# Band matrices summed into the weights' layout, and three batches convolved and transposed by halves, in a convolution and soft-mixture kernel

## The chip, the cores and the metric

One Trainium2 chip, one of its cores. The metric is the device time of one execution in microseconds (us); less is better. The kernel before was timed three times.

## The reference, cut to what matters

```python
# x [8, 3584, 192], weight [8 heads, 7], phi [192, 32], w1 [8, 192, 1024], w2 [8, 1024, 192], all float32
w = softmax(weight, axis=-1)
out = np.einsum('hk,bskhg->bshg', w, x_unf)     # causal convolution of 7 rows, one filter for each 24 channels
x = out.reshape(28672, 192)
logits = x @ phi
d = softmax(logits, axis=0)                     # over all 28672 rows
slot_input = (d.T @ x).reshape(8, 4, 192)
slot_out[e] = np.maximum(slot_input[e] @ w1[e], 0.0) @ w2[e]
c = softmax(logits, axis=1)
return c @ slot_out.reshape(32, 192)
```

## The kernel before

**The stages.** The eight batches of x (2.75 MB each) are loaded one after the other into five buffers, xs0 to xs4, each as 128 partitions x 32 windows x 192 channels; batches 5 to 7 take the buffers of batches 0 to 2. TensorE convolves a batch in place: a window of 128 rows gives 2 x 56 outputs, by a matmul with a band matrix `toep` (partitions x heads x 64) into PSUM, and ScalarE (ACT) or VectorE (DVE) copies the result back over x ("evacuation", L181 or L185). DVE transposes the convolved batch in six blocks of 32 channels into `xt` (L457, L504), TensorE multiplies the blocks by phi into the logits (L526, accumulated over the six blocks in `lg0` and `lg1`), DVE copies the logits out and takes their maximum (L541 to L556), ACT makes the exponentials (L567), TensorE turns them (L598) and multiplies them with the batch (L620, "dispatch"). The batches go through this in the groups [0], [1, 2], [3, 4], [5, 6], [7]. Beside it w1 and w2 are loaded into buffers that have come free, and the row softmax (L651 to L679) runs in gaps on POOL (GpSimd), DVE and ACT. After the last group comes the small two-layer network (L782 to L883), then the output: matmuls (L912), evacuation, and 22 MB of stores.

**The band matrix (L319 to L389).** The softmax of the weights is taken on DVE (L335 to L341). `shf` holds ones shifted along 32 columns. For each half of the heads a product of 128 x 1064 is taken (L363, one half on DVE, the other on POOL), summed over the 7 taps by DVE into a band of 4 heads x 38 columns (L366), and eight small copies by ACT, DVE or POOL put pieces of the band into `toep` (L382).

**The halo copies (L304 to L309).** Eight partitions of every quarter of a batch are copied from partitions 64 to 71 by POOL or ACT (L181, L183), in two pieces for batches 0 and 1 and in one piece for the others.

**The convolution.** `conv` (L425) takes one head at a time over the whole batch, with the two PSUM pairs cv0 and cv1 in turn. `conv_halves` (L461) is used for batch 0 alone: half of the batch (quarters 0 and 1, then 2 and 3) and two heads at a time, with four PSUM pairs; behind each half come two transposes of three blocks each (L504). `xt` has six blocks for the first batch of a group and three for the second, whose blocks 3 to 5 are written over its blocks 0 to 2 after their logits.

**The order of the work.** Every step is given to a planner (`Plan`) with a cost, what it reads and writes, and a priority; it walks through the steps by these costs, chooses an engine where several are allowed, and puts out the instructions of each engine in that order. On the chip every engine then runs its own list in order. Loads are issued by SP in order; `load` lets each wait for an earlier one, so that at most `most` bytes are under way:

```python
most = 1900000 if b < 2 else 1600000
```

Four dummy matmuls (L400) keep TensorE busy before the first convolution.

## Time and profile before

| what | value |
|---|---|
| time, median of 3 runs | 209.65 us (208.44 to 210.06) |
| the profiled execution: its own time | 209.57 us |
| its span, first to last instruction | 207.7 us |
| busy: PE, DVE, ACT, POOL | 168.5, 153.4, 96.5, 101.9 us |
| DMA | 60.16 MB, mean 290 GB/s |
| mean granted clock of TensorE | 0.929 |

The span lies inside the profiled execution's own time; what is around it is 1.87 us. In the trace every float32 matmul stands as two records, so an "x32" of matmuls is 16 matmuls.

### The profile page before, as it was taken

What the parts mean: (1) busy time and instruction counts of PE and PEld (TensorE: products, weight loads), DVE (VectorE), ACT (ScalarE), POOL (GpSimd) and SP (SyncE); (2) the same over time, 40 slices, a digit from 0 to 9 for tenths busy, and PEclk for the clock granted to TensorE, in tenths of its full rate; (3) what the DMA queues carried; (4) which work ended last, traced back from release to release, by engine and by line L of the source; (5) the groups of instructions that cost most, each with busy time, mean ns of one, the idle gap of its engine ahead of it and who ended that gap; (6) DMA issues with size and microseconds to landing.
All of it is one profiled execution on the core that took longest, in us unless ns stands there. A gap on an engine that the chain in (4) does not pass through costs nothing.

```text
span 207.7 us, 6742 instructions
## 1 busy us (share of the span) xinstructions
PE 168.5 (81%) x2816; PEld 102.0 (49%) x2816; DVE 153.4 (74%) x236; ACT 96.5 (46%) x163; POOL 101.9 (49%) x115
## 2 busy tenths in 40 slices
PE   4776699999899998999998989899899996729000
PEld 2255545323254362443643557657698896618000
DVE  6999648888799887998689995975587797555100
ACT  3557237453665506848038423140497876424000
POOL 8854336566464654560800035776668668740000
PEclk9999579999999999999999999999999999685855
DMA  4999999999999989758786887880199999999994
GB/s 118 333 319 318 284 299 275 322 299 327 295 312 303 303 254 304 212 174 278 245 252 218 246 266 246 260 264 3 42 328 391 411 412 407 407 413 411 413 417 203
DMA packets 47806, 60.16 MB, mean 290 GB/s; under 512 B 2848, under 2 KB 41632, under 8 KB 47776
## 3 DMA queue, kind: packets, MB, share of 16 engines
q1 hardware_dynamic: 47776, 59.73, 86.9%
q8 instruction: 22, 0.36, 0.7%
q14 instruction: 8, 0.07, 0.1%
HBM read 37.70 MB, written 22.02 MB: 288 GB/s over the span
## 4 chain that ended last, share of the span: by engine, by line
PE 41%; DMA 30%; DVE 8%; POOL 4%; ACT 4%; issue 3%; SPq 1%; POOLq 1%; DVEq 0%; ACTq 0%
DMA xs<-in_x_dram 25%; PE cv L436 10%; PE lg L526 7%; PE cv L620 5%; PE cv L912 4%; PE lg L598 4%; DMA out_dram<-xs 3%; PE lg L620 3%; PE lg L866 3%; ACT xs L181 3%; PE lg L912 2%; DMA xs<-in_moe_w_dram 2%; DVE xs L185 2%; PE cv L826 2%; POOL eall L663 2%
## 5 line engine op out<-in xcount | busy, mean ns | idle before, releaser
L181 ACT COPY xs<-cv 128x768 f32<-128x768 f32 (+1 forms) x60 | 46.2, 796 | 57.1 <-PE cv L436 29.3
L183 POOL COPY xs<-xs 8x1536 f32<-8x1536 f32 (+1 forms) x32 | 41.4, 1297 | 34.3 <-DMA xs<-in_x_dram 32.7
L457 DVE STREAM_TRANSPOSE xt<-xs 128x1024 f32<-128x1024 f32 x42 | 49.0, 1214 | 1.6 <-issue 0.8
L436 PE MATMUL cv<-xs,toep 64*64 64x384 f32 x448 | 44.4, 500 | 3.8 <-ACT xs L181 2.1
L185 DVE COPY xs<-cv 128x768 f32<-128x768 f32 (+1 forms) x32 | 29.8, 939 | 13.1 <-PE cv L912 6.6
L663 POOL TENSOR_TENSOR eall<-eall,rms 128x896 f32<-128x896 f32 x16 | 26.9, 1698 | 24.1 <-DVE rms L651 17.1
L526 PE MATMUL lg<-xt,phi 32*32 32x448 f32 (+1 forms) x960 | 30.0, 512 | 3.2 <-DVE xt L504 2.5
L912 PE MATMUL cv<-so,eall 32*128 32x192 f32 x248 | 25.2, 460 | 8.0 <-DVE eall L671 7.2
L436 PEld LDWEIGHTS cv<-xs,toep 64*64 64x64 f32 x448 | 13.2, 131 | 28.5 <-ACT xs L181 11.1
L912 PEld LDWEIGHTS cv<-so,eall 32*128 32x128 f32 x248 | 20.5, 317 | 10.5 <-issue 7.8
L526 PEld LDWEIGHTS lg<-xt,phi 32*32 32x32 f32 x960 | 15.1, 109 | 15.1 <-issue 4.8
L912 PE MATMUL lg<-so,eall 32*128 32x192 f32 x200 | 20.6, 433 | 0.0
L671 DVE STREAM_TRANSPOSE eall<-eall 128x896 f32<-128x896 f32 x16 | 17.4, 1096 | 2.1 <-POOL eall L663 1.9
L912 PEld LDWEIGHTS lg<-so,eall 32*128 32x128 f32 x200 | 18.1, 319 | 0.5 <-ACT xs L181 0.3
L654 POOL TENSOR_TENSOR tree<-eall 128x448 f32<-128x448 f32 x8 | 9.2, 1149 | 13.6 <-ACT eall L675 13.6
L185 DVE COPY xs<-lg 128x768 f32<-128x768 f32 (+2 forms) x24 | 12.8, 558 | 3.1 <-PE lg L846 2.0
L541 DVE TENSOR_SCALAR_CACHE_REDUCE eall<-lg 128x448 f32<-128x448 f32 x16 | 9.1, 621 | 7.6 <-PE lg L526 7.6
L181 ACT COPY xs<-lg 128x768 f32<-128x768 f32 (+1 forms) x20 | 13.6, 707 | 1.9 <-PE lg L912 1.6
L675 ACT ACTIVATE eall<-eall 128x896 f32<-128x896 f32 x8 | 7.6, 955 | 10.8 <-POOL eall L663 10.6
L620 PE MATMUL cv<-xs,dn 128*32 128x192 f32 x256 | 11.5, 328 | 1.1 <-issue 0.7
L620 PE MATMUL lg<-xs,dn 128*32 128x192 f32 x256 | 11.6, 328 | 0.3 <-ACT dn L181 0.3
L658 POOL TENSOR_TENSOR tree<-tree 128x224 f32<-128x224 f32 (+2 forms) x24 | 10.9, 452 | 1.9
(97 smaller groups left out, 180.4 us busy)
## 6 DMA issues: line engine op xcount, KB each, us to landing
xs<-in_x_dram SPq DMA_DIRECT2D x56, 384.0 KB, 5.1
out_dram<-xs SPq DMA_DIRECT2D x28, 672.0 KB, 10.3
xs<-in_moe_w_dram SPq DMA_DIRECT2D x16, 256.0 KB, 4.7
xt<-in_moe_w_dram SPq DMA_DIRECT2D x16, 192.0 KB, 3.5
xs<-in_moe_w_dram SPq DMA_DIRECT2D x16, 192.0 KB, 3.8
xs<-in_x_dram SPq DMA_DIRECT2D x8, 288.0 KB, 4.6
out_dram<-xs SPq DMA_DIRECT2D x3, 768.0 KB, 5.6
xs<-in_moe_w_dram SPq DMA_DIRECT2D x4, 512.0 KB, 4.7
```

The lines of the kernel that those rows point to most:

```text
L181: nc.scalar.copy(dst, src)
L183: nc.gpsimd.tensor_copy(dst, src)
L185: nc.vector.tensor_copy(dst, src)
L436: nc.tensor.matmul(cv[k][64 * g : 64 * g + 64, hf, 0 : NI * CG].rearrange("p (c i d) -> p c i d", c=4, d=CG), toep[r, h, :], xv[r, g, :, : ...
L457: nc.vector.transpose(xt[:, NB + k % NR if i else k], xs[s][:, :, 32 * k : 32 + 32 * k])
L526: nc.tensor.matmul(lg[a // 2][32 * c : 32 * c + 32, a % 2, 0 : nm_ * n].rearrange("p (m u j) -> p m u j", m=nm_, j=TB), phi4[r, k, :], xt[ ...
L620: nc.tensor.matmul(dp[32 * c : 32 * c + 32, 0:D], dn[:, u, 32 * c : 32 * c + 32], xs[s][:, U * c + u, :], start=(u == 0), stop=(u == U - 1),)
L654: nc.gpsimd.tensor_tensor(out=tree, in0=ev[:, :, 0:w], in1=ev[:, :, w:], op=op)
L658: nc.gpsimd.tensor_tensor(out=dst, in0=tree[:, :, 0:w], in1=tree[:, :, w : 2 * w], op=op)
L663: return lambda e: veng(e).tensor_tensor(out=ev, in0=ev, in1=rb, op=op)
L671: turn = lambda e: nc.vector.transpose(eall[:, b], eall[:, b])
L912: nc.tensor.matmul(banks[c][:, (q - k) * D : (q - k + 1) * D], cb[r, :, q], so[r, :], start=True, stop=True, tile_position=(32 * c, 0),)
```

## The change

The products and sums of the band are laid out as `toep` itself: `onehot` (three DVE copies out of the identity) holds for each partition a one where its column is, a product of two heads x 56 columns x 7 taps is 128 x 784, and the sum over the taps is written straight to `toep`, so that the small copies are gone. There are four such products, on DVE and POOL in turn, and matmuls wait for the two heads that they use. Batches 1 and 2 are convolved by `conv_halves` too, batch 1 with the PSUM pairs cv0 and cv1, batch 2 with cv0, cv1 and lg1; the transposes behind each half take two blocks at a time. In batch 0 a dummy matmul stands behind each half. Halo copies are in two pieces for batches 0 to 2, each waits for its own piece of the load, and only in batch 0 may ACT take them. `most` is 1,900,000 for batch 2 as well, and the planner's rate for loads is 300 GB/s instead of 315.

```diff
-    def dma(nbytes, rate=315e3):
+    def dma(nbytes, rate=300e3):
...
-    shf = sb("shf", P, 32 + 2 * ZS)
+    TW = T + ZS
+    onehot = sb("onehot", P, TW)
...
-        most = 1900000 if b < 2 else 1600000
+        most = 1900000 if b < 3 else 1600000
...
-            if b < 2:
-                halves = (("POOL", "ACT"), i0, im), (("POOL", "ACT"), im, i1)
-            else:
-                halves = ((("POOL",), i0, i1),)
-            for j, (es, a0, a1) in enumerate(halves):
+            for j, (a0, a1) in enumerate(((i0, im), (im, i1)) if b < 3 else ((i0, i1),)):
                 add(
                     lambda e, a0=a0, a1=a1: copy(e, xv[0:NH, a0:a1, :], xv[64 : 64 + NH, a0:a1, :]),
-                    {en: 0.1 + (a1 - a0) * D * 0.0009 for en in es}, reads=[xsk[s][k], f"z{s}"], writes=[f"{xsk[s][k]}.{j}"], prio=b * 10 - 30,
+                    {en: 0.1 + (a1 - a0) * D * 0.0009 for en in (("POOL", "ACT") if b < 1 else ("POOL",))},
+                    reads=[f"{xsk[s][k]}.r{i}" for i in ((j,) if b < 3 else (0, 1))] + [f"z{s}"],
+                    writes=[f"{xsk[s][k]}.{j}"] if b < 3 else [f"{xsk[s][k]}.{i}" for i in range(2)], prio=b * 10 - 30,
                 )
...
     def shifts(e):
-        nc.vector.tensor_reduce(
-            out=shf[:, ZS : ZS + 32], in_=ident.rearrange("p (g n) -> p n g", n=32), axis=AX.X, op=ALU.add
+        o = ZS - PRE
+        nc.vector.tensor_copy(onehot[0:64], ident[0:64, -o : TW - o])
+        nc.vector.tensor_copy(onehot[64:P], ident[64:P, 64 + NH - ZS : 64 + NH - ZS + TW])
+        nc.vector.tensor_copy(onehot[0:NH, TW - NH : TW], ident[0:NH, 0:NH])
...
+    nt = T * KT
+    for i in range(H // 2):
+        h0 = 2 * i
+        prod = fe[:, h0 * nt : (h0 + 2) * nt]
+
+        def bprod(e, prod=prod, h0=h0):
+            w_ = wv[:, h0 : h0 + 2, :].unsqueeze(2).broadcast_to((P, 2, T, KT))
+            oh = bass.AP(onehot.tensor, onehot.offset, ap=[onehot.ap[0], [0, 2], [1, T], [1, KT]])
+            veng(e).tensor_tensor(out=prod.rearrange("p (h c k) -> p h c k", h=2, k=KT), in0=oh, in1=w_, op=ALU.mult)
+
+        def bsum(e, prod=prod, h0=h0):
+            nc.vector.tensor_reduce(
+                out=toep[:, h0 : h0 + 2, :].rearrange("p h (a c) -> p (h a) c", c=32)[:, :, 0:TB],
+                in_=prod.rearrange("p (b c k) -> p b c k", b=4, k=KT), axis=AX.X, op=ALU.add,
+            )
...
-    for i in range(4):
+    def zeros(reads, prio, cost):
         add(
             lambda e: nc.tensor.matmul(
                 cv[0][:, 0, :], ident, dT[0].rearrange("p u a j -> p (u a j)")[:, 0:512], start=True, stop=True
             ),
-            {"PE": 1.36}, reads=["ident", "dT0"], writes=["cv0"], prio=-100,
+            {"PE": cost}, reads=["ident", "dT0", *reads], writes=["cv0"], prio=prio,
         )
+
+    for i in range(4):
+        zeros((), -100, 1.36)
...
-    def conv_halves(b):
+    def conv_halves(b, pr, bufs, keys, xts):
...
-            kb = NB // 2
-            for i in range(2):
+            if b == 0:
+                zeros(["half0"], pr, 0.9)
+            ns = xts[1]
+            for k0 in range(0, ns, 2):
+                kn = min(2, ns - k0)
...
-    conv_halves(0)
+    conv_halves(0, 0, cv + lg, ["cv0", "cv1", "lg0", "lg1"], (0, NB))
...
-                conv(nxt[j], pr + 10 + 10 * j)
-                turns(nxt[j], j, pr + 14 + 10 * j, range(NR if j else NB))
+                if nxt[j] < 3:
+                    conv_halves(nxt[j], pr + 10 + 10 * j, cv + lg[1:] * j, ["cv0", "cv1"] + ["lg1"] * j, (j, NR if j else NB))
+                else:
+                    conv(nxt[j], pr + 10 + 10 * j)
+                    turns(nxt[j], j, pr + 14 + 10 * j, range(NR if j else NB))
```

In the lists of the engines xs_85 to xs_89 are the buffers xs0 to xs4, cv_63 and cv_64 are cv0 and cv1, lg_65 and lg_66 are lg0 and lg1. The start of DVE's list, before, from the identity to the weights' softmax:

```order
L344 TENSOR_REDUCE shf<-ident 128x32
L415 TENSOR_REDUCE par<-ident 128x2
L416 TENSOR_REDUCE gsel<-ident 128x32
L418 COPY gsel<-gsel 128x32 x3
L335 TENSOR_REDUCE small<-wb 128x8
```

And now:

```order
L344 COPY onehot<-ident 64x62
L345 COPY onehot<-ident 64x62
L346 COPY onehot<-ident 8x8
L401 TENSOR_REDUCE par<-ident 128x2
L402 TENSOR_REDUCE gsel<-ident 128x32
L404 COPY gsel<-gsel 128x32 x3
L334 TENSOR_REDUCE small<-wb 128x8
```

Three copies stand where one reduction stood, ahead of everything else that DVE does there. DVE's list before, from the first product of the band to the transposes of batch 0 (the second product is on POOL):

```order
L363 TENSOR_TENSOR eall<-shf,wb 128x1064
L366 TENSOR_REDUCE eall<-eall 128x152
L185 COPY toep<-eall 32x4x22
L185 COPY toep<-eall 32x4x16
L185 COPY toep<-eall 32x4x30
L185 COPY toep<-eall 32x4x8
L366 TENSOR_REDUCE eall<-eall 128x152
```

```order
L185 COPY xs_85<-cv_63 128x2x8x48
L185 COPY xs_85<-lg_65 128x2x8x48
L185 COPY xs_85<-lg_66 128x2x8x48
L504 STREAM_TRANSPOSE xt<-xs_85 128x3x512
L185 COPY xs_85<-cv_64 128x2x8x48
L504 STREAM_TRANSPOSE xt<-xs_85 128x3x512 x3
```

And now (the second and the fourth product are on POOL):

```order
L361 TENSOR_TENSOR eall<-onehot,wb 128x784
L364 TENSOR_REDUCE toep<-eall 128x4x28 x2
L361 TENSOR_TENSOR eall<-onehot,wb 128x784
L364 TENSOR_REDUCE toep<-eall 128x4x28 x2
L185 COPY xs_85<-lg_65 128x2x8x48
L185 COPY xs_85<-lg_66 128x2x8x48
L494 STREAM_TRANSPOSE xt<-xs_85 128x2x512 x6
```

DVE's copies into `toep` are gone, a second product and two more sums have come to it, and of batch 0's evacuations it has two instead of four; ACT has the other six. TensorE's list before, from the last convolutions of batch 1 (xs_86) through batch 2 (xs_87) to the first logits of the two:

```order
L436 MATMUL cv_64<-xs_86,toep 64x384 x4
L620 MATMUL lg_65<-xs_85,dn 32x192 x16
L436 MATMUL cv_63<-xs_87,toep 64x384 x4
L436 MATMUL cv_64<-xs_87,toep 64x384 x4
L436 MATMUL cv_63<-xs_87,toep 64x384 x4
L436 MATMUL cv_64<-xs_87,toep 64x384 x4
L436 MATMUL cv_63<-xs_87,toep 64x384 x4
L526 MATMUL lg_65<-xt,phi_70 32x448 x8
L526 MATMUL lg_66<-xt,phi_70 32x448 x8
L436 MATMUL cv_64<-xs_87,toep 64x384 x4
L436 MATMUL cv_63<-xs_87,toep 64x384 x4
```

And now:

```order
L466 MATMUL cv_64<-xs_86,toep 64x8x24 x8
L611 MATMUL lg_65<-xs_85,dn 32x192 x32
L466 MATMUL cv_63<-xs_87,toep 64x8x24 x8
L466 MATMUL cv_64<-xs_87,toep 64x8x24 x8
L466 MATMUL lg_66<-xs_87,toep 64x8x24 x8
L466 MATMUL cv_63<-xs_87,toep 64x8x24 x8
L466 MATMUL cv_64<-xs_87,toep 64x8x24 x8
L466 MATMUL lg_66<-xs_87,toep 64x8x24 x8
L466 MATMUL cv_63<-xs_87,toep 64x8x24 x8
L466 MATMUL cv_64<-xs_87,toep 64x8x24 x8
L517 MATMUL lg_65<-xt,phi_70 32x448 x8
L517 MATMUL lg_66<-xt,phi_70 32x448 x8
```

All of batch 2 now stands ahead of the first logits of batches 1 and 2, and all of these logits ahead of batch 3, where before three of batch 2's eight heads and one of batch 3's stood among them. The list of SP, which issues the loads, has the same transfers in the same order as before.

## Rows read from the trace of the kernel before

**Rows 1.** The span in 40 slices of 5.19 us; PEclk is the granted clock in tenths
```profile
PE   4776699999899998999998989899899996729000
...
PEclk9999579999999999999999999999999999685855
DMA  4999999999999989758786887880199999999994
```

**Rows 2.** The chain that ended last: start us, us, what (a transfer from issue to landing)
```profile
3.19 6.08 DMA xs<-in_x_dram
9.29 4.98 DMA xs<-in_x_dram
```

**Rows 3.** Timeline of the start: start us, us, engine, line, operation, out<-in, count [idle before <-releaser]
```profile
1.97 1.85 POOL L393 MEMSET dT<- 128x1024 f32 x2
...
2.48 1.73 DVE L418 COPY gsel<-gsel 128x32 f32<-128x32 f32 x3
...
4.22 0.21 DVE L335 TENSOR_REDUCE small<-wb 128x8 f32<-128x56 f32 x1
...
5.93 1.27 DVE L363 TENSOR_TENSOR eall<-shf,wb 128x1064 f32<-128x1064 f32 x1
6.06 3.48 POOL L363 TENSOR_TENSOR eall<-shf,wb 128x1064 f32<-128x1064 f32 x1 [1.26 <-DVE wb L341]
...
8.61 2.85 DVE L185 COPY toep<-eall 32x88 f32<-32x88 f32 x4
...
12.78 0.66 DVE L185 COPY toep<-eall 32x88 f32<-32x88 f32 x3
...
13.47 0.96 DVE L185 COPY xs<-cv 128x768 f32<-128x768 f32 x1
...
14.31 0.78 ACT L181 COPY xs<-cv 128x768 f32<-128x768 f32 x1
```

**Rows 4.** Timeline: last dummy, batch 0's second half, its transposes and logits, batch 1's first convolutions
```profile
8.44 0.59 PE L400 MATMUL cv<-dT,ident 128*128 128x512 f32 x1
...
15.92 1.64 PE L480 MATMUL cv<-xs,toep 64*64 64x192 f32 x32 [0.75 <-POOL xs L183]
...
18.96 5.08 DVE L504 STREAM_TRANSPOSE xt<-xs 128x1536 f32<-128x1536 f32 x3
...
22.43 5.98 PE L526 MATMUL lg<-xt,phi 32*32 32x224 f32 x188 [2.53 <-DVE xt L504]
...
28.35 1.52 PE L436 MATMUL cv<-xs,toep 64*64 64x384 f32 x16
```

**Rows 5.** Timeline, batches 1 to 4 (L183: the halo copy of a batch's last quarter)
```profile
35.69 1.46 POOL L183 COPY xs<-xs 8x1536 f32<-8x1536 f32 x1 [1.02 <-DMA xs<-in_x_dram]
...
38.96 1.52 PE L436 MATMUL cv<-xs,toep 64*64 64x384 f32 x16
...
43.40 1.05 PE L526 MATMUL lg<-xt,phi 32*32 32x448 f32 x32
...
46.08 1.46 POOL L183 COPY xs<-xs 8x1536 f32<-8x1536 f32 x1 [0.89 <-DMA xs<-in_x_dram]
...
49.20 1.20 DVE L457 STREAM_TRANSPOSE xt<-xs 128x1024 f32<-128x1024 f32 x1
...
52.98 1.52 PE L436 MATMUL cv<-xs,toep 64*64 64x384 f32 x16
...
56.43 1.46 POOL L183 COPY xs<-xs 8x1536 f32<-8x1536 f32 x1 [0.95 <-DMA xs<-in_x_dram]
...
63.05 1.52 PE L436 MATMUL cv<-xs,toep 64*64 64x384 f32 x16
```

**Rows 6.** Timeline: the last batch's logits; a POOL and a DVE operation side by side
```profile
119.67 3.59 PE L526 MATMUL lg<-xt,phi 32*32 32x224 f32 x176 [0.19 <-ACT dn L181]
...
128.73 1.16 POOL L654 TENSOR_TENSOR tree<-eall 128x448 f32<-128x448 f32 x1
...
129.28 0.66 DVE L769 TENSOR_TENSOR gtmp<-gmin,gsel 128x32 f32<-128x32 f32 x1
```

More of the change, by code (lines that the diff above doesn't have):

```diff
@@ L343, in shifts @@
     def shifts(e):
-        nc.vector.tensor_reduce(
-            out=shf[:, ZS : ZS + 32], in_=ident.rearrange("p (g n) -> p n g", n=32), axis=AX.X, op=ALU.add
-        )
-    add(shifts, {"DVE": 0.2}, reads=["ident"], writes=["shf"], prio=-60)
-    add(softmax_w, {"DVE": 2.2}, reads=["wb"], writes=["wb"], prio=-50)
-    BW = 32 + ZS
-    fe = eall.rearrange("p a b -> p (a b)")
-    band = fe[:, 0 : H * BW].rearrange("p (h c) -> p h c", c=BW)
-    HG = H // 2
-    for i in range(2):
-        h0, h1 = i * HG, (i + 1) * HG
-        prod = fe[:, (H + h0 * KT) * BW : (H + h1 * KT) * BW].rearrange("p (h c k) -> p h c k", c=BW, k=KT)
-        def bprod(e, prod=prod, h0=h0, h1=h1):
-            w_ = wv[:, h0:h1, :].unsqueeze(2).broadcast_to((P, HG, BW, KT))
-            sh = bass.AP(shf.tensor, shf.offset, ap=[shf.ap[0], [0, HG], [1, BW], [1, KT]])
-            veng(e).tensor_tensor(out=prod, in0=sh, in1=w_, op=ALU.mult)
-        def bsum(e, prod=prod, h0=h0, h1=h1):
-            nc.vector.tensor_reduce(out=band[:, h0:h1, :], in_=prod, axis=AX.X, op=ALU.add)
-        n = HG * BW * KT
-        add(bprod, {"POOL": pool(n)} if i else {"DVE": dve(n)}, reads=["wb", "shf"], writes=[f"prod{i}", f"e0.{i}"], prio=-42 + i)
-        add(bsum, {"DVE": dve(n)}, reads=[f"prod{i}"], writes=[f"band{i}"], prio=-40 + i)
-        for a, (p0, rows, off, blks) in enumerate((
-            (0, 32, -PRE, (0,)), (0, NH, T - NH, (1,)), (32, 32, 32 - PRE, (0, 1)),
-            (64, 32, -NH, (0, 1)), (96, 32, 32 - NH, (0, 1)),
-        )):
-            for k in blks:
-                t0, t1 = max(TB * k, off), min(TB * k + 32, off + BW)
-                def bput(e, p0=p0, rows=rows, off=off, h0=h0, h1=h1, t0=t0, t1=t1, k=k):
-                    sl = slice(p0, p0 + rows)
-                    copy(e, toep[sl, h0:h1, t0 + (32 - TB) * k : t1 + (32 - TB) * k], band[sl, h0:h1, t0 - off : t1 - off])
-                m = HG * (t1 - t0)
-                add(
-                    bput, {"ACT": act(m), "DVE": dve(m), **({"POOL": 0.15 + m * 0.0011} if i else {})}, reads=[f"band{i}", "tz"],
-                    writes=[f"toep{i}.{a}.{k}"], prio=-40 + i,
-                )
@@ L389, in tile_conv_softmoe @@
-    toepk = [[f"toep{i}.{a}.{k}" for a, k in ((0, 0), (1, 1), (2, 0), (2, 1), (3, 0), (3, 1), (4, 0), (4, 1))] for i in range(2)]
+        o = ZS - PRE
+        nc.vector.tensor_copy(onehot[0:64], ident[0:64, -o : TW - o])
+        nc.vector.tensor_copy(onehot[64:P], ident[64:P, 64 + NH - ZS : 64 + NH - ZS + TW])
+        nc.vector.tensor_copy(onehot[0:NH, TW - NH : TW], ident[0:NH, 0:NH])
+    add(shifts, {"DVE": 0.4}, reads=["ident"], writes=["onehot"], prio=-60)
+    add(softmax_w, {"DVE": 2.2}, reads=["wb"], writes=["wb"], prio=-50)
@@ new lines, in tile_conv_softmoe @@
+    fe = eall.rearrange("p a b -> p (a b)")
+    nt = T * KT
[10 more added lines that the diff above has]
+                in_=prod.rearrange("p (b c k) -> p b c k", b=4, k=KT), axis=AX.X, op=ALU.add,
+            )
+        add(
+            bprod, {"POOL": pool(2 * nt) + 0.1} if i % 2 else {"DVE": dve(2 * nt) + 0.05}, reads=["wb", "onehot"],
+            writes=[f"prod{i}", f"e0.{i % 2}"], prio=-42 + i,
+        )
+        add(bsum, {"DVE": dve(2 * nt) + 0.05}, reads=[f"prod{i}", "tz"], writes=[f"toep{i}"], prio=-41.5 + i)
@@ L491, in conv_halves @@
                 add(
-                    mm, {"PE": 0.8}, reads=[f"{xsk[s][c]}.{j}" for c in cs for j in range(2)] + [f"z{s}"] + toepk[h0 // HG],
-                    writes=[keys[k]], prio=pr,
+                    mm, {"PE": 0.8}, reads=[f"{xsk[s][c]}.{j}" for c in cs for j in range(2)] + [f"z{s}"] + [f"toep{h0 // 2}"],
+                    writes=[keys[k], f"half{b}"], prio=pr,
                 )
@@ L498, in conv_halves, with tr @@
                 )
[L499 to L508 removed]
+            if b == 0:
[3 more added lines that the diff above has]
+                kn = min(2, ns - k0)
+                def tr(e, us=us, k0=k0, kn=kn):
+                    v = xs[s][:, us, 32 * k0 : 32 * (k0 + kn)]
+                    x0 = k0 + (NB if xts[0] else 0)
+                    nc.vector.transpose(xt[:, x0 : x0 + kn, us, :], v.rearrange("p u (k d) -> p k u d", k=kn))
+                add(
+                    tr, {"DVE": dve(2 * U * kn * 32)},
+                    reads=[xck[s][h][c] for h in range(32 * k0 // CG, (32 * (k0 + kn) - 1) // CG + 1) for c in cs],
+                    writes=[xtk[xts[0]][kk][c] for kk in range(k0, k0 + kn) for c in cs], prio=pr + (4 if b else 1),
                 )
```

39 lines of the change are left out of this document (15 added, 24 removed).

## The prediction

> **What bounds the kernel now.** I read the slices first, then the chain, then the timeline stage by stage. In the slices [rows 1] the reader is to see three stretches. From about 31 to 145 us PE stands at 8 to 9 tenths and more: TensorE sets the pace. From about 156 us to the end DMA stands at 9 in every slice but the last: the stores set it. [...]
>
> The chain gives the arrivals of batch 0: the piece issued at 3.19 lands at 9.27 (end of the first half), the one issued at 9.29 at 14.27 (end of the second) [rows 2]. Four pieces in 5.0 us: batch 1's first half is there by about 20.
>
> The timeline of the start shows what is late today. The band's first product and sum are done before 8.61, but four small DVE copies then take 2.85 us, where three of the same kind later take 0.66 [rows 3]: the slow ones run beside POOL's product (6.06 to 9.54) and what follows it. Only then come the evacuations (from 13.47). The second half is convolved from 15.92 to about 18.9; the last three transposes run from 18.96 to 24.04, and the logits stand idle 2.53 us, start at 22.43 and end at 28.4, where batch 1 begins, at 28.35 [rows 4]. [...]
>
> **The band, step by step.** Removed: a reduction, two products and two sums of 1064 columns, sixteen small copies. Added: three `onehot` copies, four products (two on DVE, two on POOL) and four sums (DVE) of 784 columns.
>
> The copies. The nearest row is the three `gsel` copies of 32 columns: 1.73 us from 2.48, while POOL zeroes dT from 1.97 to 3.82 and then other tiles [rows 3]. They wait, their work is small. The `onehot` copies stand still earlier in DVE's list, and I let them wait the same way until about 4.1. Behind them come two reductions and the `gsel` copies; the softmax's seven small operations take 1.7 from 4.22 to 5.93, 0.25 each, so these three take 0.75, with a tenth for the hand-over 0.85: the softmax starts at 4.95 instead of 4.22. So 0.75 late; bounds 0 (they slip in at once and `gsel` waits as today) and 1.0.
>
> Products and sums. Softmax 1.7, done at 6.65. A DVE product of 784 is 1.27 x 784/1064 = 0.94; a sum the same (the present one lies between 7.20 and 8.61). POOL's product took 3.48 for 1064, of which 1.14 lay beside DVE's product; if it stood still then, it needs 2.34, and 1.72 for 784 [rows 3]. First product to 7.6, first sum to 8.55; POOL's first from 7.6 to 9.35, its sum to 10.3, POOL's second from 9.35 to 11.1. DVE's second product is due at 10.3, beside POOL's. Does it run? A DVE product of 32 elements took 0.66, from 129.28 to 129.94, and ended right behind POOL's 128.73 + 1.16 = 129.89 [rows 6]: so it waits, to 11.1. Then the product to 12.05, sums to 13.0 and 13.95.
> [...]
>
> **Batch 0.** TensorE has heads 0 to 3 from about 10.15 (landing 9.27 plus a halo copy), the third pair at 13.05, the fourth from 14.0 to 14.8. The dummy: one record took 0.59 [rows 4], two make a matmul, between 0.6 and 1.2; I take 0.9, to 15.7. The second half is ready at 14.27 plus a 0.8 halo copy = 15.1, so the dummy delays it by 0.6, and it ends at 15.7 + 4 x 0.82 = 19.0, no earlier than today. (0.82: a record group of 1.64 is two steps [rows 4].) What the new order gains is on DVE: two evacuations of 0.96 [rows 3] behind the sums, to 15.9, then six transposes of 1.20 (the row of 1024 elements [rows 5]) without a gap: first half to 19.5, second to 20.7, 21.9, 23.1. The second half's four evacuations are all on ACT (0.78 each [rows 3]) and end at 19.8, in time. Logits start at 20.7, six steps of 0.65 at the upper clock: 24.6, against 28.35. Gain 3.75. Two steps (1.3) take longer than a transpose (1.2), so TensorE does not wait again.
>
> **Batches 1 and 2.** From 28.35 to 38.96 TensorE needs 10.6 for batch 1 with the exponentials' transposes and the dispatch [rows 4, 5]. Halved, a step costs 0.82 instead of 0.76 (1.52 for two heads): 0.06 more, 16 times, 1.0 us in both batches. With 0.4 of it here, batch 2 begins at 24.6 + 11.0 = 35.6. Its second half is loaded: the last quarter's copy runs 35.69 to 37.15 [rows 5], due is 35.6 + 3.3 = 38.9. Its convolution ends at 35.6 + 6.6 = 42.2; the logits' first block needs six of the eight steps (40.5), an evacuation 0.78 and a transpose 1.20: 42.5. Six blocks of 1.05 [rows 5]: 48.8. The second group of three transposes is written over the first, block by block behind its logits, 1.20 against 1.05 each, and hides but for some tenths. Batch 3 then starts at 48.8 with all 8 heads; it is loaded at 46.08 + 1.46 = 47.54 [rows 5]. Today it goes on at 52.98 with 7 left, which is 8 at 52.2. **Gain 3.4.**
>
> **What follows.** From there the work is the same and TensorE bound [rows 1]. Batch 4 is loaded at 57.89 and starts at 63.05 [rows 5], 5.2 later, so its load is early enough. The weights: DMA falls to 0 in the slice from 140 to 145, all loads have landed, while the network ends about 147; 3.4 earlier leaves them in time even if they don't move. The stores are bound by DMA and start when the network ends, so they move with it; DMA is full without a break to the end, so there is a backlog that covers a row softmax which moves less. Planner rate and `most`: SP's list is the same and DMA is full there, I take 0.
>
> Sum: the profiled execution's 209.57, which stands at the median 209.65, minus 3.4: **206.2**.
>
> **Rivals.** [...]
> *The lower clock stays.* The logits at 6.1 instead of 3.92 lose 2.2: 208.4. For it: TensorE still waits about 1 us at 19.9 and in three places before. Against: before its fall today it idled 2.5 us, and a dummy now stands in two of the gaps.
> *The gain is swallowed further on* (a chain of row softmax on POOL, or the weights): about 209. Against it: the slack above.
> *Slower.* The lower clock grips in batches 1 and 2 too: their halved steps hang on two PSUM pairs and an evacuation of 0.78 to 0.96 each, with holes. Two stretches as long as today's (about 6.8 us, from the digits 5 and 7) take 6.8 us of half speed, less what hides behind evacuations, 5.8, against the gain of 3.4: 212. It decides from a loss of 3.4 on. Against it: the clock stood at 9 through today's batches 1 and 2 with the same holes.
>
> **How the numbers follow.** The forecast 0.55 (its own range 205.4 to 207.2, from 0 to 1.0 for the copies and 0.6 to 1.2 for the dummy); no blocking 0.20; lower clock 0.14; swallowed 0.05; slower 0.06. The range from 204.4 (the cap, with 0.5 for the noise of the three runs) to 208.6 (the lower clock) leaves out the last two. A measurement can tell 1% here, about 2.1 us: below 207.55 lie the first two, 0.74; between, 0.20; slower 0.06.
>
> **What would show it.** Right: no DVE copies into `toep`; the softmax of the weights starts near 5.0; the second DVE product ends about 1 us behind POOL's; logits of batch 0 begin near 20.7 and end near 24.6 with the clock at 9 throughout; batch 3's convolution starts near 48.8; the first stores stand some 3.4 us earlier, as does the end. Wrong: a 5 in PEclk before 35 us, logits that wait for transposes, a wait for DMA ahead of batch 3, or a gain at 49 us that is not there at 146.

## The result and the profile after

The kernel before took 209.66 us (median of 20 runs, 207.59 to 211.98), the changed kernel 207.38 us (20 runs, 204.82 to 212.02). The ratio is 0.9882 with a 95% interval of 0.985 to 0.9914: 2.5 us faster, 1.8 to 3.1. (Ratios, here and below, leave out executions more than 1.5% above the fastest of their kernel, so they need not be the ratio of the medians.) The prediction was 206.2 us with a range of 204.4 to 208.6.

The execution profiled with this result took 209.75 us. What follows reads the profile of another execution of the same kernel, 206.57 us with a span of 204.8 (run e1_after below).

The slices of that profile, as in [rows 1], each 5.12 us:

```profile
PE   4969969999899998999988879899899999960000
PEclk9987999999999999999999999999999999995555
DMA  4999999999999949679577778883099999999993
```

In the start PE now stands at 4 9 6 9 9 6 9 where it stood at 4 7 7 6 6 9 9; the 6 in the sixth slice (25.6 to 30.7 us) is new. The dip of the granted clock has moved from the fifth and sixth slice, where the logits of batch 0 ran, to the third and fourth (8 and 7, 10 to 20 us), where their convolution runs. The timeline of DVE and POOL in the start, which answers to [rows 3] (columns as there):

```profile
1.53 2.39 DVE L344 COPY onehot<-ident 64x62 f32<-64x62 f32 x1 [0.66 <-POOL ident masks.py:199]
1.90 1.84 POOL L376 MEMSET dT<- 128x1024 f32 x2
...
5.10 0.20 DVE L334 TENSOR_REDUCE small<-wb 128x8 f32<-128x56 f32 x1
...
6.80 0.98 DVE L361 TENSOR_TENSOR eall<-onehot,wb 128x784 f32<-128x784 f32 x1
6.93 4.43 POOL L361 TENSOR_TENSOR eall<-onehot,wb 128x784 f32<-128x784 f32 x2 [2.15 <-DVE wb L340]
7.89 0.97 DVE L364 TENSOR_REDUCE toep<-eall 128x112 f32<-128x784 f32 x1
...
10.43 1.76 DVE L361 TENSOR_TENSOR eall<-onehot,wb 128x784 f32<-128x784 f32 x1
...
12.23 1.85 DVE L364 TENSOR_REDUCE toep<-eall 128x112 f32<-128x784 f32 x2
```

The band is done at 12.23 + 1.85 = 14.08. The first copy stands for 2.39 us beside POOL's zeroing, where its sister behind it takes 0.21 (L345, at 3.94); the second DVE product takes 1.76 where the first took 0.98, and ends after POOL's at 11.36. The sum at 7.89, beside the same POOL products, is not held up: 0.97, against 0.92 for each of the two sums behind those products.

TensorE's timeline from there to batch 3, which answers to [rows 4, 5], with DVE's transposes:

```profile
15.61 2.07 PE L383 MATMUL cv<-dT,ident 128*128 128x512 f32 x2
16.60 3.49 DVE L494 STREAM_TRANSPOSE xt<-xs 128x1024 f32<-128x1024 f32 x3
17.61 1.53 PE L466 MATMUL cv<-xs,toep 64*64 64x192 f32 x32
...
20.28 3.50 DVE L494 STREAM_TRANSPOSE xt<-xs 128x1024 f32<-128x1024 f32 x3 [0.19 <-POOL xs L183]
20.37 1.12 PE L383 MATMUL cv<-dT,ident 128*128 128x512 f32 x2
21.43 3.87 PE L517 MATMUL lg<-xt,phi 32*32 32x224 f32 x192
...
25.23 0.87 PE L466 MATMUL cv<-xs,toep 64*64 64x192 f32 x14
27.55 1.19 PE L466 MATMUL cv<-xs,toep 64*64 64x192 f32 x18 [1.45 <-issue]
...
37.56 1.53 PE L466 MATMUL cv<-xs,toep 64*64 64x192 f32 x32
...
43.09 6.83 PE L517 MATMUL lg<-xt,phi 32*32 32x448 f32 x192
...
49.86 1.64 PE L422 MATMUL cv<-xs,toep 64*64 64x384 f32 x16
```

The line to look at is the one at 27.55. Batch 1's first convolution breaks off after 14 of 32 records, in the middle of a step whose operands are all there, and goes on 1.45 us later; "issue" means that it waited for nothing that the profile names. The kernel before has no such line there.

The gain against the profile before, followed through the span (the last logits begin at 117.67 with 160 records in 3.38; the stores are issued by SP):

| | before | after | gain |
|---|---|---|---|
| logits of batch 0 end | 28.4 | 25.3 | 3.1 |
| batch 2 begins | 38.96 | 37.56 | 1.4 |
| batch 3 begins, 8 heads left | 52.2 | 49.86 | 2.3 |
| last batch's logits end | 123.26 | 121.05 | 2.2 |
| first store issued | 149.00 | 147.46 | 1.5 |
| end of the span | 207.7 | 204.8 | 2.9 |

So 1.7 of the 3.1 us are gone before batch 2, some of it comes back, and 1.4 us come from the stores, which the change does not touch. One profile of each kernel stands behind this table, and profiles of one kernel differ: in a second one of the kernel before (e11 below) batch 2 begins at 37.99 and the first store at 148.11, which leaves gains of 0.4 and 0.65; in the one taken with the result the break at the same record takes 2.49 us, the granted clock is at its lower level (0.50; the upper one is 1.00) from 28.6 to 32.0 us behind it, and batch 3 begins at 52.21.

### The profile page after: what moved, and what is told of

Read it like the earlier page. It is cut to its first block, busy times and chain, and to the rows that moved or that the text cites. A ratio compares the mean times of both kernels' runs of the same rounds, so it can differ in the third digit from the quotient of the medians.

```text
span 208.0 us, 7001 instructions
## 1 busy us (share of the span) xinstructions
PE 170.6 (82%) x2948; PEld 107.8 (52%) x2948; DVE 151.0 (73%) x234; ACT 96.4 (46%) x158; POOL 104.0 (50%) x118
## 4 chain that ended last, share of the span: by engine, by line
PE 43%; DMA 30%; DVE 7%; issue 4%; ACT 2%; SPq 2%; POOL 1%; DVEq 0%; POOLq 0%; ACTq 0%
DMA xs<-in_x_dram 30%; PE cv L906 11%; PE cv L422 6%; PE lg L906 5%; PE lg L517 5%; PE cv L611 4%; PE lg L589 3%; PE lg L611 3%; PE lg L860 3%; DVE xs L185 2%; PE cv L820 2%; SPq L251 2%; ACT xs L181 2%; POOL xs L183 1%; DVE eall L532 1%
## 5 line engine op out<-in xcount | busy, mean ns | idle before, releaser
L183 POOL COPY xs<-xs 8x1536 f32<-8x1536 f32 (+1 forms) x37 | 43.2, 1180 | 18.4 <-DMA xs<-in_x_dram 14.4
L443 DVE STREAM_TRANSPOSE xt<-xs 128x1024 f32<-128x1024 f32 x33 | 38.3, 1211 | 1.1 <-PE lg L517 0.7
L185 DVE COPY xs<-cv 128x768 f32<-128x768 f32 (+1 forms) x28 | 26.0, 938 | 13.3 <-PE cv L466 4.2
L422 PE MATMUL cv<-xs,toep 64*64 64x384 f32 x320 | 31.9, 499 | 2.9 <-DVE xs L185 1.9
L517 PE MATMUL lg<-xt,phi 32*32 32x448 f32 (+1 forms) x960 | 27.4, 470 | 0.2 <-ACT dn L181 0.2
L422 PEld LDWEIGHTS cv<-xs,toep 64*64 64x64 f32 x320 | 10.1, 131 | 20.0 <-DVE xs L185 6.5
L517 PEld LDWEIGHTS lg<-xt,phi 32*32 32x32 f32 x960 | 13.5, 103 | 11.7 <-issue 3.7
L466 PE MATMUL cv<-xs,toep 64*64 64x192 f32 x288 | 17.2, 365 | 2.8 <-issue 2.5
L494 DVE STREAM_TRANSPOSE xt<-xs 128x1024 f32<-128x1024 f32 (+1 forms) x16 | 17.6, 1150 | 1.2 <-POOL xs L183 0.8
L466 PEld LDWEIGHTS cv<-xs,toep 64*64 64x64 f32 x288 | 11.6, 148 | 9.1 <-issue 5.3
L185 DVE COPY xs<-lg 128x384 f32<-128x384 f32 (+2 forms) x25 | 13.3, 558 | 2.4 <-PE lg L840 2.0
```

The costliest lines, as they stand in the source:

```text
L183: nc.gpsimd.tensor_copy(dst, src)
L185: nc.vector.tensor_copy(dst, src)
L422: nc.tensor.matmul(cv[k][64 * g : 64 * g + 64, hf, 0 : NI * CG].rearrange("p (c i d) -> p c i d", c=4, d=CG), toep[r, h, :], xv[r, g, :, : ...
L443: nc.vector.transpose(xt[:, NB + k % NR if i else k], xs[s][:, :, 32 * k : 32 + 32 * k])
L466: nc.tensor.matmul(ov[:, h], toep[r, h0 + h, :], xv.rearrange("p (c g i) d -> p g c i d", c=2, g=2)[:, g], start=True, stop=True,)
L494: nc.vector.transpose(xt[:, x0 : x0 + kn, us, :], v.rearrange("p u (k d) -> p k u d", k=kn))
```

## The experiments

Every run was made beside the kernel before on the same chip. The ratio is to the kernel before, with its 95% interval.

| run | median us | ratio |
|---|---|---|
| e1_after | 206.31 | 0.9848 (0.9794 to 0.9903) |
| e2_bands | 207.98 | 0.9954 (0.9919 to 0.999) |
| e3_nodummy | 206.19 | 0.9866 (0.9827 to 0.9905) |
| e4_onehot_act | 206.86 | 0.9855 (0.9802 to 0.9907) |
| e5_whole12 | 206.83 | 0.9871 (0.9821 to 0.9921) |
| e6_before_busy | 209.21 | 0.9986 (0.9949 to 1.0023) |
| e7_most | 220.93 | 1.0503 (1.0428 to 1.0577) |
| e8_both | 205.39 | 0.9826 (0.9775 to 0.9877) |
| e9_mixed | 206.56 | 0.9871 (0.9817 to 0.9926) |
| e10_both_whole | 205.9 | 0.9767 (0.97 to 0.9834) |
| e11_before | 208.66 (one run) | |
| e12_bands_again | 208.76 (one run) | |

**The changed kernel again.** No edit.

> The changed kernel again, unaltered, for a profile on a chip with all clocks undisturbed and for its time beside the variants of this call. Theory 1 (TensorE's instructions arrive late): logits of batch 0 end near 25, then TensorE stands still for 1 us or more within the first matmuls of batch 1, shown as issue, behind a packet of the instruction queue, so that batch 2's convolution starts later than 38 in place of the 35.6 of the prediction; gain 2 to 3 us against before. Rival 2 (lower clock alone): no such standstill once the clock is at 9 in the first 35 us; batch 2 starts near 36 and the gain is 3.4 or more. Rival 3 (halo copies and zero rows on POOL): TensorE waits, but named for POOL, ahead of batch 2 or batch 3.

Measured: the standstill is there, with the clock at its upper level (9 in all slices from 20.5 to 184 us, 1.00 from 20 to 54 us). Batch 2 starts at 37.56, in between; the gain is 3.2 us in this series. Rival 2, the clock alone, foretold no standstill, and no wait for POOL stands ahead of batch 2 or batch 3, as rival 3 had it.

**No matmuls on zeros behind the halves.**

```diff
-            if b == 0:
-                zeros(["half0"], pr, 0.9)
```

> The changed kernel without the two matmuls on zeros behind batch 0's halves. Rival 2 (the dummy at the lower clock delays the second half): the second half starts up to 1 to 2 us earlier, logits of batch 0 start about 1 us earlier, time 0.5 to 1 us less than the changed kernel. If instead the dummy keeps the clock up: the granted clock is lower during the logits, they take over 5 us and the time is 1 to 2 us more. Theory 1: where the logits come earlier at full speed, the standstill behind them grows by as much and the time is the same within 0.5.

The same time. The second half does start earlier and the logits end at 24.38 instead of 25.30, at the upper clock (1.00 from 0 to 54 us). TensorE's rows behind the logits:

```profile
20.66 3.72 PE L515 MATMUL lg<-xt,phi 32*32 32x224 f32 x188 [1.98 <-DVE xt L492]
24.31 1.19 PE L466 MATMUL cv<-xs,toep 64*64 64x192 f32 x18
26.48 1.52 PE L466 MATMUL cv<-xs,toep 64*64 64x192 f32 x30 [0.98 <-issue]
```

This run gives more than it was made for. Without the 4 matmul records of the two dummies the break comes 4 records later in the convolution, after 18 instead of 14. Counted in TensorE's own list it is the same place: 8 + 128 + 4 + 192 + 14 = 346 matmul records, and 8 + 128 + 192 + 18 = 346; with the weight load of each, 692. It is a place in the list of instructions, not in the work.

What stands at such places is in the list of DMA queues. The changed kernel's row and that of the kernel before:

```profile
q8 instruction: 23, 0.38, 0.7%
```

```profile
q8 instruction: 22, 0.36, 0.7%
```

22 packets of 16 KB go with 2816 matmul and 2816 weight load records, on average 256 records for each packet. The times of the packet ahead of the break, read from the trace of each run, with the record at which TensorE stood still (counted in the order in which records start) and how long after the packet's end it went on:

```
run               packet          record  goes on  after its end  waited
e1_after          25.23 to 26.11  692     27.55    1.44           1.45
e3_nodummy        24.26 to 25.19  692     26.47    1.28           0.98
e4_onehot_act     22.82 to 23.74  692     25.27    1.53           0.83
e5_whole12        24.57 to 25.51  691     26.97    1.46           0.97
e6_before_busy    27.45 to 28.39  687     29.76    1.37           1.19
e7_most           29.03 to 29.95  692     31.36    1.41           1.90
e8_both           22.89 to 23.77  692     25.34    1.57           0.46
```

In seven kernels, two of them with fewer instructions ahead of the logits and two with another convolution behind them, the break stands at records 687 to 692 and ends 1.28 to 1.57 us behind the packet. In the profile taken with the result it does so too (record 692, 1.34 behind, 2.49 waited). In the four profiles with the lower clock in batch 0's logits and the logits in one piece (the kernel before twice, e12, e10; 188 records in 5.98, 5.11, 6.00 and 5.02 us) there is no break marked "issue" there. That TensorE waits there for its own instructions is the reading that fits all of these places; no run changed the packets themselves.

**One-hot copies on ScalarE.**

```diff
-        nc.vector.tensor_copy(onehot[0:64], ident[0:64, -o : TW - o])
+        nc.scalar.copy(onehot[0:64], ident[0:64, -o : TW - o])
...
-    add(shifts, {"DVE": 0.4}, reads=["ident"], writes=["onehot"], prio=-60)
+    add(shifts, {"ACT": 0.7}, reads=["ident"], writes=["onehot"], prio=-60)
```

> The changed kernel with the three one-hot copies on ScalarE, so that VectorE's softmax does not stand behind a copy that POOL holds up. Softmax starts near 4.3 instead of 5.3, sums are done about 0.8 earlier, near 13.4. Theory 1: logits of batch 0 end at most 0.8 earlier and the standstill behind them takes what is won; same time within 0.5. Rival 3 (start of batch 0 carries through): 0.8 less than the changed kernel.

The first copy and the softmax's first reduction, in the timeline:

```profile
2.14 0.23 ACT L344 COPY onehot<-ident 64x62 f32<-64x62 f32 x1
...
4.19 0.21 DVE L334 TENSOR_REDUCE small<-wb 128x8 f32<-128x56 f32 x1 [1.26 <-DMA wb<-in_weight_dram]
```

ScalarE's copy takes 0.23 beside the same POOL zeroing that made DVE's take 2.39, and the softmax starts 0.9 earlier, waiting only for the weights. The sums are done at 13.16 instead of 14.08, the logits end at 23.64. The time is the same, as theory 1 had it, but not for its reason. The logits ended 1.7 earlier (the clock stayed up ahead of the second half, too: the dummy took 1.12), the break did not take that back but was shorter, 0.83, and batch 2 begins at 35.27, 2.3 earlier than in e1. Of these, 1.7 are left at batch 3 (48.13) and 0.7 at the first store (146.78): they are lost further on, and what takes them was not followed up.

**Batches 1 and 2 whole.**

```diff
-                if nxt[j] < 3:
+                if nxt[j] < 1:
```

> The changed kernel with batches 1 and 2 convolved and transposed whole, as in the kernel before; batch 0 as changed. If the halving of batches 1 and 2 is worth something: logits of 1 and 2 end later than the 49.9 of the changed kernel, by up to 1 to 2 us, and the time is 0.5 to 1.5 more. By the steps of the prediction it costs 1.0 of longer steps and gives back the last transposes: the same time within 0.5. The standstill at record 692 of TensorE's list stays (theory 1), only that other matmuls stand there.

The same time. From the end of batch 0's logits to batch 2, without the standstill, halves take 37.56 - 25.30 - 1.45 = 10.8 us and whole batches 36.16 - 24.57 - 0.97 = 10.6; the last transposes then give back about 0.4 in batch 2 (12.3 from there to batch 3 against 12.7: whole, one head of batch 3 is already done at 49.62, which is 48.8 with all eight left). Halving batches 1 and 2 is worth nothing that these runs can tell.

**The new band alone.** The kernel before with `onehot`, the four products and the four sums; everything else as it was.

> The kernel before with the new construction of the band alone (three one-hot copies, four products, four sums), the rest as before. By my working the sums are done near 14.2, where the last small copy of before ended near 13.5: the construction alone is no gain. Expected within 1 us of before (0 to +1), logits of batch 0 still ending at 28 to 29.5. Rival: the four blocked copies were what held batch 0, then the logits end by 26.5 and the whole gain of 2 to 3 us stands here.

Faster by 0.5% (0.1 to 0.8), less than half of the change's 1.2%; the expectation was 0 to 1 us more, and it is about 1 us less. The profiled execution took 206.58 us and had the clock up throughout the start (1.00 from 0 to 54 us):

```profile
21.92 3.67 PE L511 MATMUL lg<-xt,phi 32*32 32x224 f32 x188 [2.52 <-DVE xt L489]
...
27.43 2.29 PE L421 MATMUL cv<-xs,toep 64*64 64x384 f32 x16 [0.40 <-ACT xs L181]
...
36.60 1.52 PE L421 MATMUL cv<-xs,toep 64*64 64x384 f32 x16
```

So the kernel was profiled a second time:

> The kernel with the new band alone again, for a second profile. Its first profile was its fastest execution, with the clock up throughout the start (batch 0's logits 3.67 us, batch 2 from 36.6), while its median lies only 1.5 us below before. If the lower clock usually takes its logits: about 6 us for 188 records, no standstill behind them, batch 2 from 38 to 39. If not: as the first profile, and the time is lost elsewhere.

Second profile, batch 0's logits and the start of batch 2:

```profile
22.10 6.00 PE L511 MATMUL lg<-xt,phi 32*32 32x224 f32 x188 [2.52 <-DVE xt L489]
...
38.64 1.52 PE L421 MATMUL cv<-xs,toep 64*64 64x384 f32 x16
```

That is the start of the kernel before, 0.3 us earlier [rows 4, 5]. The band alone moves little there; the transposes that follow it hold the logits until 22.1.

The two profiles are of one kernel and differ in the clock: at its lower level from 21.2 to 28.0 us in the second, at its upper level in the first (188 records of logits in 6.00 and in 3.67 us). The logits end at 25.59 instead of 28.10, batch 2 begins at 36.60 instead of 38.64, the first store is issued at 146.54 instead of 148.59, and the span is 204.8 instead of 207.0. So of the 2.5 us at the end of the logits (2.3 by the clock, 0.2 by an earlier start) 2.0 are still there at the first store. It is one profile of each. The break is there too: TensorE goes on at record 693 at 28.20, 1.46 behind its packet (25.57 to 26.74), but it had to wait for an evacuation until 27.43 anyway, and little is lost.

**The kernel before with a busy TensorE.** Two matmuls on zeros behind batch 0's second half; nothing else.

```diff
+        for i in range(2):
+            add(
+                lambda e: nc.tensor.matmul(
+                    cv[0][:, 0, :], ident, dT[0].rearrange("p u a j -> p (u a j)")[:, 0:512], start=True, stop=True
+                ),
+                {"PE": 0.9}, reads=["ident", "dT0", "half0"], writes=["cv0"], prio=pr,
+            )
```

> The kernel before, with only two matmuls on zeros put behind batch 0's second half, where TensorE waits 2.5 us for the transposes. Rival 2 (the clock): if in most executions of before the lower clock takes batch 0's logits, they run in 3.9 instead of 6.0 here, and the time falls by 1 to 2 us. If the drop in the profile of before was one execution's chance, the time is that of before within 0.5. Theory 1: where the logits run at the upper clock, a standstill appears at record 692 plus or minus a few, behind a packet of the instruction queue, of 0.4 to 1.5 us, that the profile of before does not have.

```profile
18.89 1.98 PE L513 MATMUL cv<-dT,ident 128*128 128x512 f32 x4
...
23.42 3.72 PE L534 MATMUL lg<-xt,phi 32*32 32x224 f32 x188 [2.05 <-DVE xt L504]
27.07 1.50 PE L436 MATMUL cv<-xs,toep 64*64 64x384 f32 x11
29.76 1.51 PE L436 MATMUL cv<-xs,toep 64*64 64x384 f32 x13 [1.19 <-issue]
...
39.59 1.52 PE L436 MATMUL cv<-xs,toep 64*64 64x384 f32 x16
```

The clock stays up in the logits, 3.72 us instead of 5.98, and the time does not move: 0.9986, interval 0.9949 to 1.0023. In place of the slow logits stands the break that the kernel before does not have, and batch 2 begins no earlier than in [rows 5]. But the logits also began 1.0 later than before: in this profile the granted clock was at its lower level from 12.7 to 16.1 us, in batch 0's convolution (30 records in 2.99 us from 13.35, 31 in 1.48 from 17.48), and the last transposes began 1.0 later. So matmuls on zeros in this gap win nothing. That the lower clock in the logits, which the prediction priced at 2.2 us, costs nothing does not follow; the two profiles of the band alone say otherwise, and so does the kernel before again:

> The kernel before again, for a second profile of it. If the lower clock in batch 0's logits is usual: 188 records of logits in about 6.0 us again. If it was chance: 3.7 us, the logits end near 26.3 and a standstill of 0.4 to 1.5 us follows near record 690. The way from the first store to the end, 58.7 us in the first profile against 57.3 in the changed kernel: the same 58.7 if it belongs to the kernel, 57.3 if it was chance.

```profile
22.43 5.11 PE L526 MATMUL lg<-xt,phi 32*32 32x224 f32 x188 [2.54 <-DVE xt L504]
27.47 1.52 PE L436 MATMUL cv<-xs,toep 64*64 64x384 f32 x16
29.39 1.72 PE L436 MATMUL cv<-xs,toep 64*64 64x384 f32 x16 [0.39 <-ACT xs L181]
```

The clock falls in the same logits, from 23.9 to 27.3 us instead of 21.4 to 28.2 (0.50): 188 records in 5.11 us instead of 5.98. They end 0.9 earlier than in the first profile (27.55 against 28.42), and that lasts: batch 2 begins at 37.99 instead of 38.96, the first store stands at 148.11 instead of 149.00, the span is 206.9 instead of 207.7. No break follows, because the second pair of heads waits for an evacuation until 29.39, and the packet (25.99 to 26.94) is 2.45 us old by then. The way from the first store to the end is 206.9 - 148.11 = 58.8 again: that belongs to the kernel.

**Fewer loads in flight.**

```diff
-        most = 1900000 if b < 3 else 1600000
+        most = 1000000 if b < 3 else 1600000
```

> The changed kernel with at most 1.0 MB of x loads in flight for the first three batches in place of 1.9 MB. If the instruction packet comes late because it stands behind queued loads: it lies earlier behind TensorE's entry into the block before, the standstill at record 692 falls from 1.3 to 1.8 us to below 0.8. If the packet's lateness has another cause, the standstill is 1.2 or more as before. The time: the same within 1 unless the loads themselves become late, then 1 to 3 more with waits for DMA ahead of batches 1 to 3.

```profile
GB/s 119 187 204 214 213 149 213 206 173 311 319 274 296 335 326 291 270 303 253 282 224 253 214 241 258 273 232 254 8 71 377 410 422 416 419 420 419 424 423 193
```

```profile
24.96 3.69 PE L517 MATMUL lg<-xt,phi 32*32 32x224 f32 x192
28.59 0.87 PE L466 MATMUL cv<-xs,toep 64*64 64x192 f32 x14
31.36 1.19 PE L466 MATMUL cv<-xs,toep 64*64 64x192 f32 x18 [1.90 <-issue]
```

The break is 1.90, no shorter: with fewer loads in flight the packet came no earlier, 4.07 us behind the first record of the logits (29.03 - 24.96) instead of the 3.80 of e1 (25.23 - 21.43); why it comes when it does stays open. The price was larger than expected: 187 to 214 GB/s in the second to fifth slice where the changed kernel moves 321 to 367, and 10 us in the time against the kernel before.

**Both edits of the start, and the convolution mixed into the logits.** e8 joins the edits of e3 and e4; e9 also gives batch 1's convolution a priority ahead of batch 0's logits.

```diff
-                    conv_halves(nxt[j], pr + 10 + 10 * j, cv + lg[1:] * j, ["cv0", "cv1"] + ["lg1"] * j, (j, NR if j else NB))
+                    conv_halves(nxt[j], pr + (10 if ci else -1) + 10 * j, cv + lg[1:] * j, ["cv0", "cv1"] + ["lg1"] * j, (j, NR if j else NB))
```

> The changed kernel with both edits: one-hot copies on ScalarE and no matmuls on zeros behind the halves. If the gains at batch 0's logits add up (1.0 and 1.7 of 25.3), they end near 22.8. Theory 1: the standstill at record 692 takes back at most 1.5 of it; logits of 1 and 2 end near 47.5 and the time is 0.5 to 1.5 less than the changed kernel's. If the x loads are the bound by then: a wait for DMA ahead of batch 3 and no more than 0.5.

> As the one before, and batch 1's convolution placed ahead of the logits of batch 0 in the planner's order of priority, so that its steps stand between the logits' blocks and TensorE's list has no dense stretch of 192 small matmuls. Theory 1: the standstill at record 692 (1.3 to 1.8 us with the logits in one piece) falls below 0.4, batch 2's convolution starts 1 to 2 us earlier than the 37.6 of the changed kernel and 0.5 to 1.5 earlier than in the kernel with both edits. If the standstill is not from the density of the list, it stays above 1.0 at the same record.

e8 is the best of this series with 205.39, and its interval overlaps that of the changed kernel. Its logits end at 23.77, so the gains of the two edits did not add up to the 22.8 expected; the break is down to 0.46, and batch 3 begins at 47.35 against 49.86; no wait for DMA ahead of it. Of these 2.5 us little is left in that profile at the first store (147.22): in the last batch, where 192 records of small logits matmuls are again followed by a dispatch, its break is longer than in the changed kernel (1.86 against 1.03), and the 57 records behind it take 4.07, where 57 take 2.60 in the kernel before at a clock of 1.00:

```profile
118.45 0.53 PE L609 MATMUL cv<-xs,dn 128*32 128x192 f32 x7
120.84 4.07 PE L609 MATMUL cv<-xs,dn 128*32 128x192 f32 x57 [1.86 <-issue]
```

In e9 the list is mixed:

```profile
24.07 0.69 PE L515 MATMUL lg<-xt,phi 32*32 32x224 f32 x32
24.69 1.53 PE L466 MATMUL cv<-xs,toep 64*64 64x192 f32 x32
26.15 1.42 PE L515 MATMUL lg<-xt,phi 32*32 32x224 f32 x64
27.50 1.53 PE L466 MATMUL cv<-xs,toep 64*64 64x192 f32 x32
```

Record 692 passes at 26.93 with no wait; the packet ended at 25.23. The break is gone where the list is not dense, as theory 1 says. That the density alone did it is not shown: counted from record 436 (256 ahead of 692), TensorE reached record 688 after 3.6 us instead of the 2.8 of e1, but the packet also began sooner, 0.8 us behind record 436 instead of 2.4. The time is not better than e8's: batch 0's logits now end at 29.6, and its exponentials, their evacuation (0.79) and the sum into `acc` (1.13, ahead of the logits at 43.45) are waited for instead. The profiled execution took 210.51 us, with the lower clock from 19.9 to 23.3 us (60 records of logits in 2.19 us there, 64 in 1.42 from 26.15) and a break of 2.64 in the last batch, so it does not show what decides the median.

**Both edits, batches 1 and 2 whole.**

> One-hot copies on ScalarE, no matmuls on zeros behind the halves, and batches 1 and 2 whole as in the kernel before: what is left of the change is the band, and batch 0's transposes two blocks at a time. If halving batches 1 and 2 is worth nothing, 205.4 as the kernel with both edits, within 0.7; if it is worth what the whole steps save (0.25 to 1.0), down to 204.5; if the halves were worth something, 0.7 or more above 205.4.

205.9, within 0.7 of e8: the halves are not needed. With `onehot` on ScalarE, no dummies and whole batches the ratio to the kernel before is the lowest of all runs, 0.97 to 0.9834; whether it beats the changed kernel, whose interval over 20 runs is 0.985 to 0.9914, was not tried side by side.

## Why the prediction was right, step by step, and where two errors met

The time came out inside the range, 1.2 us above the value in the first series and 0.1 in the second. The steps, from the profile of e1_after:

| step | predicted | measured |
|---|---|---|
| softmax of the weights starts | 4.95 | 5.10 |
| sums done | 13.95 | 14.08 |
| dummy behind the first half | 0.9 | 2.07 |
| second half starts, ends | 15.7, 19.0 | 17.61, 20.44 |
| transposes end | 23.1 | 23.78 |
| logits of batch 0 | 20.7 to 24.6 | 21.43 to 25.30 |
| batch 2 begins | 35.6 | 37.56 |
| batch 3 begins | 48.8 | 49.86 |
| gain at the end | 3.4 | 2.9 |

**The band** was right in each wait. The copy and the second product stood behind POOL as the prediction read from [rows 3, 6] (the second product ended at 12.19, 0.83 behind POOL's), while the sum at 7.89 took 0.97 beside POOL's products. The 0.20 for no blocking, a DVE that runs on beside POOL, fell with 2.39 for the first copy. The cap behind the lower end of the range, 204.4, is an estimate from [rows 5]: batch 3, loaded at 47.54, can start 4.7 us ahead of 52.2, which gives 204.9, less 0.5. No run here met it: e8 begins batch 3 at 47.35 with no wait for DMA ahead of it.

**The step on batch 0** was mis-sized in two terms. The dummy, bounded by 0.6 and 1.2 from a row at the upper clock [rows 4], took 2.07, because the granted clock was at its lower level from 14.2 to 17.6 us (0.79 in the mean from 12 to 20 us, 1.00 before and behind); the second half's row at 17.61 shows no idle time ahead of it, so the dummy is what it stood behind. The rival of the lower clock had named the right mechanism at the wrong place. In two other kernels with the dummies (e4, e5) the clock stayed up there and the dummy took 1.12. The other term, 0.82 for a step of the convolution, was too long: it is half of the 1.64 of a record group [rows 4], whose end overlaps the next group; in the same trace that one begins at 17.24, 1.32 behind 15.92. In e1 the second half's four steps took 2.83 instead of 3.3. The logits' 0.65 for a step, 3.92 for all six, is worked out from [rows 6], 176 records in 3.59 us at a granted clock of 1.00, and the 6.1 of the lower clock from the 5.98 for 188 records of [rows 4], at 0.50; e1 took 3.87 for 192 at 1.00.

**The step that failed is "With 0.4 of it here, batch 2 begins at 24.6 + 11.0 = 35.6".** Its 11.0 for the work is right: 37.56 - 25.30 - 1.45 = 10.8. What it lacked is the wait for instructions, 1.45 us. The prediction took that stretch from a profile in which the clock was low in the logits before it; there the packet came in time, or was covered by an evacuation. With the logits in 3.9 us instead of 6.0, records are used up sooner than the next packet arrives: from record 436 to 688 it took 2.8 us in e1 and 5.7 in the kernel before (0.4 of it the wait for an evacuation), while in e1 TensorE went on only 4.7 us after record 436. That also corrects the reading of [rows 4]: in this profile the logits ended 3.1 earlier, 1.0 from their earlier start (21.43 instead of 22.43) and 2.1 from the clock, and the break took 1.45 of it back. The clock's part is not lost in general: in the band alone 2.0 of 2.5 us lasted, where an evacuation stood in the place of the break.

**The step "the second group ... hides but for some tenths", 13.2 us from batch 2 to batch 3,** was too long by 0.9: 49.86 - 37.56 = 12.3 us. The 0.82 of a step is again what was mis-sized: batch 2's eight steps run from 37.56 to 43.09, 0.69 each, where 0.82 were taken; the six blocks of logits took 6.83 instead of 6.3. With 0.69 a halved step is no longer than a whole one (two heads of the kernel before follow each other in 1.45), so the 1.0 us that the prediction set down for the halves was not there; they cost little and win little (e5).

**"From there the work is the same"** failed twice, in both directions. By the first store 0.8 of the 2.3 us were lost, 0.3 of it between the first output matmul and the first store and 0.3 to the same kind of break in the last batch, first after, then before:

```profile
122.53 2.80 PE L611 MATMUL cv<-xs,dn 128*32 128x192 f32 x61 [1.03 <-issue]
```

```profile
124.44 2.60 PE L620 MATMUL cv<-xs,dn 128*32 128x192 f32 x57 [0.72 <-issue]
```

The stores, taken as bound by DMA and moving with the network, ran 57.3 us from first issue to end instead of 58.7:

```profile
147.46 4.13 SPq L928 DMA_DIRECT2D out_dram<-xs  x4
```

```profile
149.00 4.46 SPq L934 DMA_DIRECT2D out_dram<-xs  x4
```

The rate, by a window well inside the stores (the last two columns are DMA share and GB/s), first of the changed kernel, then of the kernel before:

```profile
165.00:170.00 5.00, 4.99 (x68) 4.71 (x68) 4.58 (x6) 4.04 (x6) 3.94 (x3) 1.00 1.02 417
```

```profile
165.00:170.00 5.00, 4.84 (x66) 4.55 (x61) 4.54 (x7) 4.21 (x7) 4.02 (x5) 1.00 1.02 410
```

Counted from each kernel's own first store, 400 against 380 GB/s moved from 5 to 10 us behind it, and from 10 to 50 us behind it 415 to 425 against 404 to 416: the difference is larger in the beginning, but it goes on.

The nine profiles of kernels made from the changed one (e1, e3, e4, e5, e7, e8, e9, e10 and the one of the result) have 57.2 to 57.7 us from first store to end, the five of kernels made from the one before (the kernel before twice, e2, e6, e12) 58.3 to 58.8. So the difference belongs to the kernels; its cause was not tried and stays open. Without it the gain would have been 1.5 us, and the time 208.1, still inside the range: that the value was met so closely, 0.1 us in the second series, is luck, since the missing wait and the shorter stores cancel.

**What the gain consists of.** The band alone brings 0.1 to 0.8%, everything but the halved batches 1 and 2 brings 0.8 to 1.8%. By the middle values batch 0's new order behind the band (transposes by two blocks, halo pieces that wait for their own load, dummies) and the stores are thus the larger part. The new order was not run without the band, so how much the two need each other is not shown. A rival is left: the changed kernel may win by the clock rather than by its earlier logits. The clock was up in batch 0's logits in e1, e3, e4, e5 and e8 (188 or 192 records in 3.72 to 3.89 us), but in neither profile of the kernel before (188 in 5.98 and 5.11); and with the clock up the band alone (e2) reached its first store at 146.54 and a span of 204.8, where e1 has 147.46 and 204.8. That the earlier logits can win by themselves is seen in e10: there the lower clock lies on the logits for 3.4 us as in e11 (188 records in 5.02 and 5.11 us), they begin at 19.75 instead of 22.43, and batch 2 begins at 36.06 instead of 37.99, the first store at 146.08 instead of 148.11. For the changed kernel itself, which starts them at 21.43 and then meets the break, no run parts the two. The slower rival, the lower clock in batches 1 and 2, does not hold for the profile of e1, with 9 in every slice from 20.5 us on until the stores; in the one taken with the result one such stretch, 3.4 us, fell into batch 1.

## What to carry to other kernels

When a slow stretch of TensorE is made faster, ask what it hid: here, by the reading above, a dense stretch of small matmuls ran into the arrival of its own instructions, and of the 2.1 us that the clock gave 1.45 went there. A wait marked "issue" in the middle of a step whose operands are ready, at the same count of records in kernels that differ (687 to 692 in seven of them), was what pointed to that wait; it was found by counting records from the start of the list. To learn what a clock level is worth, compare two profiles of one kernel that differ in it before building a kernel that holds the clock up. And a gain has to be followed to the last row: two errors of a prediction that cancel look like a hit.
